# Constant products into unread accumulator columns, and one batch's q and k transposed by DMA, in an attention + gated-MLP kernel

## The chip, the cores and the metric

The kernel runs on one core of one Trainium2 chip. Its metric is device time in microseconds (us) of one execution. Executions come in a faster and a slower state, so times are compared among fast runs; square brackets behind a ratio give its 95% interval. A profiled execution gives the span that the profile covers, about 1.7 us less than the run's time. Engines: TensorE (PE, with its weight loads PEld), VectorE (DVE), ScalarE (ACT), GpSimd (POOL) and SyncE (SP, which here only issues DMAs).

## The reference, cut to what matters

Four batches; eight heads of 64; 768 positions. Attention with a window of 128 and four sink positions, then a gated MLP whose gate mixes positions:

```python
scores = q @ k.T / 8            # kept where j < 4 (sink) or 0 <= i - j < 128
a = softmax(scores); x = concat_heads(a @ v)          # 768 x 512 per batch
h = gelu(x @ w_in); u, v = h[:, :512], h[:, 512:]     # input projection
v_s = w_sg @ (layernorm(v) * g_ln) + b_sg             # mixes positions
out = x + (u * v_s) @ w_out
```

## The kernel before

The kernel is one list of steps in a fixed order. Every engine runs its own instructions in the order in which the list names them; a step that waits holds up all that stand behind it on its engine. `TQ.b.p` transposes q of batch b, head pair p on PE, `EQ` evacuates it (the last letter names the engine: A, D or P), `QK` are scores, `MV`/`MU` the two halves of the input projection, `OU` output groups, `LQ`/`LK`/`LV` loads issued by POOL, `CQ`/`CK`/`CV` casts, `HM.n` means n constant products that compute nothing and keep PE's clock up.

```python
def HM(n): pre[0] = n                       # remembered, run by the next new accumulator tile
def fresh(ring, key):
    t = ring.new(key)
    for _ in range(pre[0]):                 # 512 columns each, into the tile of the next real work
        nc.tensor.matmul(t ..., iden, ks_sink[1][:, 0:512], start=True, stop=True)
    pre[0] = 0
    return t
DT = ()                                     # batches whose q and k go through DMA transposes: none
mm_ring = Ring("mm", 4, [128, 512], F32, psum)      # four accumulator tiles, in turn
q32, k32 = Ring(..., 2, F32); qn, kn = Ring(..., 2, BF16)   # the row-order path, unused before
q16, k16 = Ring(..., 3, [128, 4, NT, Dh], BF16)     # three buffers; the load casts f32 to bf16
def LQ(b, i): return rows(q32, q, b, i) if b in DT else load(q16, q, b, i)   # 2 or 4 heads a load
def turned(dst, name, src, b, p, e):        # EQ, EK
    if b in DT: return nc.sync.dma_start_transpose(out=dst.new((b, p)), in_=src[b, p])
    copy(e, dst.new((b, p)), psb((name, b, p)))      # evacuate PE's transpose
```

A buffer of a ring can be written again only when its last reader is done, so a load waits for the work that reads its buffer's previous content.

The softmax here doesn't subtract the row's maximum and nothing guards it: scores larger than these inputs give would overflow.

## Time and profile before

| | kernel before |
|---|---|
| time, median of 3 | 168.97 us (167.69 to 170.52) |
| profiled span | 165.8 us |
| first input projection, batch 0 / first MU group of batch 1 / of batch 2 / last matmul | 29.28 / 82.33 / 106.40 / 160.93 us |
| last load of q, k or v lands | 79.52 us |

I use those four moments as stage borders: **startup**, **middle** (29.28 to 106.40, in two parts) and **tail**. The row of the page that shows the DMA engines' busy tenths in 40 slices of 4.1 us, in the kernel before: loads run without a break to slice 19 (79 us).

```profile
DMA  4999999999999998799000005901110475111055
```

The table by stage for what follows the startup, kernel before (columns: start:end, length, then busy us and instructions of PE, weight load, DVE, ACT, POOL, then PE clock, DMA share, GB/s): PE is busy nearly all the time in each stage; DVE is busy 45.12 + 21.72 = 66.8 of the middle's 77.1 us.

```profile
29.28:82.33 53.05, 52.11 (x668) 32.18 (x666) 45.12 (x97) 46.50 (x57) 40.07 (x49) 1.00 1.04 223
82.33:106.40 24.07, 24.07 (x275) 14.86 (x274) 21.72 (x54) 18.74 (x23) 9.84 (x14) 1.00 0.21 47
106.40:160.93 54.53, 54.53 (x397) 30.45 (x395) 42.57 (x99) 25.93 (x30) 15.03 (x21) 1.00 0.28 81
```

### The profile page before, as it was taken

What the parts mean: (1) busy time and instruction counts of PE and PEld (TensorE: products, weight loads), DVE (VectorE), ACT (ScalarE), POOL (GpSimd) and SP (SyncE); (2) the same over time, 40 slices, a digit from 0 to 9 for tenths busy, and PEclk for the clock granted to TensorE, in tenths of its full rate; (3) what the DMA queues carried; (4) which work ended last, traced back from release to release, by engine and by line L of the source; (5) the groups of instructions that cost most, each with busy time, mean ns of one, the idle gap of its engine ahead of it and who ended that gap; (6) DMA issues with size and microseconds to landing.
All of it is one profiled execution on the core that took longest, in us unless ns stands there. A gap on an engine that the chain in (4) does not pass through costs nothing.

```text
span 165.8 us, 4047 instructions
## 1 busy us (share of the span) xinstructions
PE 154.3 (93%) x1630; PEld 90.2 (54%) x1630; DVE 131.8 (79%) x302; ACT 110.2 (66%) x132; POOL 90.4 (54%) x123
## 2 busy tenths in 40 slices
PE   5599698999899999999999999999999999999990
PEld 1253446656565677665666575545567654555530
DVE  4179979389889989987997999838999963888861
ACT  3748966949998886999879748966676404590000
POOL 8999679646896999895240394321216610212400
PEclk9959999999999999999999999999999999999999
DMA  4999999999999998799000005901110475111055
GB/s 160 199 201 255 207 210 210 203 291 218 252 244 243 261 217 267 106 240 315 10 6 0 0 4 95 255 34 63 63 63 4 95 88 211 53 65 63 0 190 190
DMA packets 23249, 24.26 MB, mean 146 GB/s; under 512 B 8000, under 2 KB 18496, under 8 KB 23232
## 3 DMA queue, kind: packets, MB, share of 16 engines
q0 software_dynamic: 12128, 14.94, 46.5%
q1 hardware_dynamic: 11104, 9.08, 18.5%
q8 instruction: 12, 0.20, 0.5%
q14 instruction: 5, 0.04, 0.1%
HBM read 24.81 MB, written 6.29 MB: 188 GB/s over the span
## 4 chain that ended last, share of the span: by engine, by line
PE 68%; DVE 2%; DVEq 0%; issue 0%
PE mm L507 19%; PE mm L524 12%; PE sc L444 9%; PE sc L486 9%; PE sc L358 6%; PE mm L308 5%; PE mm L398 3%; PE mm L404 2%; PE mm L408 2%; DVE P L373 1%; PE mm L427 1%; PE mm L344 1%; DVEq L576 0%; DVE ot L528 0%; DVE gtmp L512 0%
## 5 line engine op out<-in xcount | busy, mean ns | idle before, releaser
L366 ACT ACTIVATE P<-sc 128x1024 bf16<-128x1024 f32 (+1 forms) x48 | 44.2, 968 | 10.8 <-PE sc L358 10.7
L507 PE MATMUL mm<-wsgT,z 128*128 128x384 bf16 x192 | 33.9, 327 | 0.7 <-DVE wsgT L502 0.7
L377 POOL TENSOR_SCALAR_AFFINE_SELECT P<-P 128x512 bf16<-128x512 bf16 x21 | 14.1, 669 | 23.0 <-ACT P L366 22.8
L507 PEld LDWEIGHTS <-z 128*128 128x128 bf16 x192 | 17.9, 98 | 13.4 <-issue 2.5
L528 DVE TENSOR_TENSOR ot<-mm,x_sb 128x512 f32<-128x512 f32 x24 | 16.3, 688 | 9.0 <-PE mm L524 8.8
L524 PE MATMUL mm<-w_out_sb,wsg_gated 128*128 128x512 bf16 x96 | 23.4, 380 | 0.0
L512 DVE SCALAR_TENSOR_TENSOR gtmp<-mm,g_sb,b_bc 128x384 bf16<-128x384 f32 x32 | 19.2, 613 | 4.4 <-PE mm L507 2.8
L486 PE MATMUL sc<-xT,w_in_sb 128*128 128x384 bf16 x128 | 22.6, 326 | 0.0
L444 PE MATMUL sc<-w_in_sb,xT 128*128 128x512 bf16 x96 | 22.2, 380 | 0.0
L373 DVE TENSOR_TENSOR P<-P,mask 128x1024 bf16<-128x1024 bf16 (+1 forms) x27 | 18.9, 718 | 1.4 <-ACT P L366 1.3
L517 POOL TENSOR_TENSOR wsg_gated<-gtmp,uT 128x384 bf16<-128x384 bf16 x13 | 12.9, 998 | 12.9 <-DVE gtmp L512 11.6
L492 ACT ACTIVATE uT<-sc 128x768 bf16<-128x768 f32 x16 | 12.7, 807 | 10.4 <-PE sc L486 10.4
L199 POOL DMA_DIRECT2D v<-in_v_dram x16 | 17.0, 1064 | 4.2 <-DVE gtmp L512 1.4
L418 DVE TENSOR_TENSOR x_sb<-mm,rcp 128x384 bf16<-128x384 f32 x32 | 17.8, 558 | 1.1
L448 ACT ACTIVATE vt<-sc 128x1024 f32<-128x1024 f32 x12 | 12.3, 1025 | 8.5 <-PE sc L444 7.7
L457 DVE BATCH_NORM_STATS2 st<-vt 128x6 f32<-128x512 f32 x24 | 16.2, 674 | 2.1 <-ACT vt L448 2.0
L465 POOL TENSOR_TENSOR rs<-rs,neg_half 128x4 f32<-128x4 f32 (+1 forms) x8 | 6.9, 864 | 19.4 <-DVE rs L460 17.5
L486 PEld LDWEIGHTS <-w_in_sb 128*128 128x128 bf16 x128 | 12.3, 98 | 8.4
L398 PE MATMUL mm<-v_sb,P 128*128 128x65 bf16 x192 | 16.4, 194 | 0.2 <-DVE P L373 0.2
L398 PEld LDWEIGHTS <-P 128*128 128x128 bf16 x192 | 14.3, 98 | 4.1 <-issue 1.5
L358 PE MATMUL sc<-qT,kT 64*128 64x256 bf16 x192 | 15.5, 269 | 0.1
L404 PE MATMUL mm<-v_sb,P 128*128 128x65 bf16 x160 | 15.4, 194 | 0.0
(75 smaller groups left out, 255.1 us busy)
## 6 DMA issues: line engine op xcount, KB each, us to landing
v<-in_v_dram POOLq DMA_DIRECT2D x16, 384.0 KB, 9.6
out_dram<-ot SPq DMA_DIRECT2D x24, 256.0 KB, 2.4
q<-in_q_dram POOLq DMA_DIRECT2D x6, 384.0 KB, 11.4
k<-in_k_dram POOLq DMA_DIRECT2D x6, 384.0 KB, 12.4
wsg_gated<-in_moe_w_sg_dram POOLq DMA_DIRECT2D x1, 1152.0 KB, 14.8
w_in_sb<-in_moe_w_in_dram POOLq DMA_DIRECT2D x2, 512.0 KB, 9.0
q<-in_q_dram POOLq DMA_DIRECT2D x3, 192.0 KB, 7.0
k<-in_k_dram POOLq DMA_DIRECT2D x3, 192.0 KB, 7.4
```

Of the source, the lines that this page charges most:

```text
L199: return nc.gpsimd.dma_start(out=ring.new((b, p)).rearrange("p h t d -> p (h t) d"), in_=src[b, 2 * p:2 * p + 2].rearrange("h (t p) d -> p ...
L358: nc.tensor.matmul(sc[:, hl, 256 * jl:256 * jl + n], kT[b, p][rows, 128 * j:128 * (j + 1)], qT[b, p][rows, 128 * j:128 * j + n], start=Tru ...
L366: nc.scalar.activation(out=pt[:, :, 0:w], in_=sc_ring[b, p, g][:, :, 0:w], func=AF.Exp, scale=scale)
L373: nc.vector.tensor_mul(pt[:, :, 0:w], pt[:, :, 0:w], m.unsqueeze(1).to_broadcast([128, 2, w]))
L398: nc.tensor.matmul(av[:, il, hl, :], P[b, p, i // 2][:, hl, 256 * (i % 2):256 * (i % 2) + 128], vb[:, h, i, :], start=first, stop=False)
L404: nc.tensor.matmul(av[:, il, hl, :], P[b, p, j // 2][:, hl, 256 * (j % 2) + 128:256 * (j % 2) + 256], vb[:, h, j, :], start=False, stop=False)
L418: nc.vector.tensor_mul(xs[:, 3 * half:3 * half + 3, 128 * p:128 * (p + 1)].rearrange("p t (h d) -> p t h d", h=2), av[:, :, :, 0:Dh], rcp. ...
L444: nc.tensor.matmul(hp[:, jl, :], xT[b][:, j, c, :], w_in_sb[:, c, d_half:2 * d_half], start=(c == 0), stop=(c == KD - 1))
L486: nc.tensor.matmul(hp[:, n, 0:NH], w_in_sb[:, c, 128 * dc:128 * (dc + 1)], xT[b][:, 3 * hf:3 * hf + 3, c, :], start=(c == 0), stop=(c == K ...
L507: nc.tensor.matmul(ps[:, 0:NH], z[b][:, si, 128 * dc:128 * (dc + 1)], wsgT[:, si, NH * hf:NH * (hf + 1)], start=(si == 0), stop=(si == NT ...
L512: nc.vector.scalar_tensor_tensor(out=gtmp.new((b, hf, dc)), in0=mm_ring["g", b, hf, dc][:, 0:NH], scalar=g_sb[:, dc:dc + 1], in1=b_bc[:, N ...
L524: nc.tensor.matmul(ps, gatedT[:, (2 * b + hf) % 3, dc, 128 * tl:128 * (tl + 1)], w_out_sb[:, dc, :], start=(dc == 0), stop=(dc == KU - 1))
```

## The change

It has three intents: constant products should stop standing in front of real work; PE should lose the 96 transposes of batch 3's q and k, which DMA does instead; and the step list is a new order fitted to both.

```diff
-DT = ()
+DT = (3,)
-    q16, k16 = Ring(..., 3, ...)
+    q16, k16 = Ring(..., 2, ...)
     def HM(n):
-        pre[0] = n
+        i = (mm_ring.used - 1) % len(mm_ring.tiles)      # the tile used last
+        while i in whole:                                # tiles all of whose columns are read
+            i = (i - 1) % len(mm_ring.tiles)
+        for _ in range(n):
+            nc.tensor.matmul(mm_ring.tiles[i][:, 390:512], iden, ks_sink[1][:, 0:122], start=True, stop=True)
 ... (fresh only keeps the set `whole`; the two loads of LG change places)
 STEPS, new order. Extracts:
-... LV.1.3 LG WT.1 LQ.2.0 XE.0.2.A ... GV.0.0 LK.2.0 MV.0.1        (loads of batch 2, early)
+... EX.1.0.1 LQ.2.0 CV.1.1.P ... EQ.2.0.A LK.2.0 GT.0.1.1        (late)
-... TK.3.3 GV.1.1 TK.3.2 BN.1.0 TQ.3.2 TQ.3.3 EK.3.3.A ...
+... CQ.3.0.P ... EQ.3.0 MV.1.0 ... LQ.3.2 ... LK.3.2 CQ.3.1.D ... LK.3.3 ... LV.3.3 ...
-HM groups: 7 2 2 6 1 7 1 (26 products of 512 columns)
+HM groups: 35 6 7 2 7 21 6 1 5 5 11 4 9 9 3 12 4 5 1 (153 of 122 columns)
```

## The prediction

> **What bounds the kernel now.** I read three things in this order: the page's busy shares and slices, then one table of busy time by stage, then the chain of waits. The first two lines say that TensorE is the busy engine and nearly always at full clock; the third is the chain that ended last.
>
> ```profile
> PE 154.3 (93%) x1630; PEld 90.2 (54%) x1630; DVE 131.8 (79%) x302; ACT 110.2 (66%) x132; POOL 90.4 (54%) x123
> ...
> PEclk9959999999999999999999999999999999999999
> ...
> PE 68%; DVE 2%; DVEq 0%; issue 0%
> ```
>
> The page warns that a busy PE is not a PE at its peak, so I cut the span at the first product of each batch's input projection (29.28 us for batch 0, 75.39 for batch 1, 106.56 for batch 2, 134.38 a little before batch 3) and at the last chain product (160.48). Columns: start:end, length, then busy us (instructions) of PE, weight load, DVE, ACT, POOL, then PE clock, DMA share, GB/s.
>
> ```profile
> 0.00:29.28 29.28, 23.20 (x296) 12.75 (x297) 20.94 (x53) 19.08 (x24) 25.43 (x41) 0.94 1.06 206
> 29.28:75.39 46.11, 45.17 (x586) 28.28 (x584) 39.56 (x86) 39.83 (x50) 37.07 (x46) 1.00 1.13 234
> 75.39:106.56 31.17, 31.17 (x358) 18.86 (x356) 27.44 (x65) 25.57 (x30) 13.00 (x19) 1.00 0.27 73
> 106.56:134.38 27.82, 27.82 (x251) 16.28 (x250) 23.61 (x58) 17.46 (x20) 9.52 (x14) 1.00 0.20 60
> 134.38:160.48 26.10, 26.10 (x144) 13.88 (x142) 18.35 (x40) 8.30 (x10) 5.35 (x6) 1.00 0.34 97
> 160.48:165.80 5.32, 0.83 (x4) 0.20 (x2) 1.89 (x3) 0.00 (x0) 0.00 (x0) 0.95 0.50 187
> ```
>
> From 29.28 us on PE is busy almost without a hole. To see whether that is real work, I took the spacing of matmul starts: 216 ns for 512 columns, 163 ns for 384, 56 ns for 128, 29 ns for 65, so 2.4 columns per ns. By that rate all matmuls need 136 us, 5.5 of it the constant products. Up to 28 us there are 11.4 us of holes between the starts; from there to 160 us again only about 11.4 us, in small pieces (0.5 to 0.7 us of each 4 us while attention and MLP mix, 0.05 in the MLP alone). So there are two regimes: a **startup** of 29 us in which PE waits for loads, DVE and ACT, and 131 us in which **PE throughput** sets the pace. The last 5.3 us is the final add and store. PE work removed after 29 us should come off the time nearly one for one, as long as DVE (86%, 88%, 85% busy in the middle stages) lets it.
>
> **What the Trainium skill says.** (1) "DMA: Bandwidth & Descriptors", section "DMA Transpose (X-bar)": 2-byte types only, hence the casts; and "Rules for kernel authors" there: "A transpose next to ordinary DMAs needs nothing", so the new ones need not wait for loads. The trace has four transposes, all with no load in flight, so it gives a size and no contention. (2) "TensorE: Matmul & The Clock Gate", Part 1: the clock is halved after an idle window of about 3.4 us. The trace agrees: a record of 3.413 us at half clock from 8.5 to 11.9 us, after a window with 1.64 us of PE busy in 3.40. (3) Part 4 of that page gives about 275 ns for a transpose in context and says such work does not engage the clock. Here twelve of them take 0.36 to 0.46 us in the chain, about 31 ns each, because they pipeline; I use the measured figure.
>
> **The change, part by part.**
>
> *Batch 3's q and k leave PE.* Its 8 groups of 12 transposes are in these chain pieces (start, us, what; the first also holds one group of batch 2):
>
> ```profile
> 69.47 0.79 PE mm L308 x24
> ...
> 79.20 1.46 PE mm L308 x48
> ...
> 98.52 1.12 PE mm L308 x36
> ```
>
> Batch 3 is half of the first and all of the other two: 0.40 + 1.46 + 1.12 = **3.0 us** of PE, all on the PE-bound path. Also gone are its 8 evacuations: 6 on ACT (0.80 to 0.82 us) and 2 on DVE (0.95). Added are 8 casts of 128x768 from f32, sized by the casts of v of the same shape: 4 on DVE at 0.64 us, 2 on POOL at 0.93, 2 on ACT at 0.87, 6.2 us in all against 6.8 us of evacuations. The transposes go to SP's queue:
>
> ```profile
> xT<-x_sb SPq DMA_TRANSPOSE x4, 3.7
> ```
>
> That is 3.7 us to landing for 128x1536 bf16, with 1.4 us of issue. The new ones are half that; I estimate 2 to 3 us each, 8 x 0.75 = 6 us of issue. In the kernel before, loads end at 79 us, and batch 3's scores start at 100 us. With loads of batch 3 through a ring of two f32 buffers they may end at 85, the transposes at 92 to 95. Still hidden. Row order costs no extra DMA time per source byte: v packets (already row order) took 0.216 us for 4096 bytes, q and k packets 0.083 us for 1536 source bytes, both about 19 GB/s on an engine.
>
> *Constant products.* Before, 26 products of 512 columns write into the tile of the next real work, so they wait for it to come free and then stand ahead of that work:
>
> ```profile
> 20.99 1.67 PE L184 MATMUL sc<-ks_sink,iden 128*128 128x512 bf16 x7 [1.54 <-ACT P L366]
> 22.60 0.39 PE L358 MATMUL sc<-qT,kT 64*128 64x256 bf16 x4
> ```
>
> Seven wait 1.54 us for ACT, then run 7 x 0.215 = 1.5 us, and only then come the scores; ACT stands idle 1.39 us for them. The same happens with six at 11.95 (ACT idle 0.81) and two at 9.13 us (about 0.9). That is some 3 us of ACT idle. After, 153 products of 122 columns write columns that nobody reads, so they wait for nothing and run in the waits. They need 153 x 51 ns = 7.8 us against 5.5, but the startup has 11.4 + 5.5 = 17 us that is not real work. The half-clock window should go. I count half of the 3 us, because DVE is 98 to 100% busy from 12 to 20 us: **1.5 us**.
>
> *The order and the engines.* Three small v-sink builds (DVE, 0.17 to 0.8 plus 0.69 us each) move out of the startup into the PE-bound stages. Two output groups (4 x 216 ns each) move from before batch 2's projections to after, neutral. Counting the list with the group means: DVE +5.5 us in all (7 more casts, 4 more masks, 3 more normalisations, fewer evacuations and products), to about 137; ACT -7 to 103; POOL +5. In the stages 29 to 106 us DVE then has about 42 + 29 us of work, for about 44 + 28 us of PE time. That is tight, so I take **1.0 us** back.
>
> Sum: span 165.8 - 3.0 - 1.5 + 1.0 = 162.3 us. The profiled run's time was 167.54, 1.7 above its span: **164.0 us**.
>
> **Rivals.** (a) *DVE becomes the bound from 75 to 106 us.* For it: 88% busy already, and its work rises while PE's falls. Against: much of it can shift by some us, and ACT is relieved. It would leave the gain at 0 to 2 us, 165.5 to 167. (b) *SP's queue blocks.* The transposes of batch 2's activations stand behind the 8 new ones, and those behind casts and late loads. If the last landed after about 100 us, PE would wait at batch 2's projection for the difference; for it the ring of two; against, some 20 us of slack between the end of loads and that use. Time 166 to 169. (c) *The startup gains nothing*, because loads bound it (DMA share above 1 from 4 us to 64 us): 165.5. (d) *The startup gains all*, clock and 3 us of ACT idle: 161.5 to 162.5.
>
> **Range and chances.** The runs before lie at 167.69, 168.97 and 170.52, wide for a fast state; I guess the startup clock differs from run to run, which denser products would steady, in favour of the change. Against the median of 168.97, 2% is 165.6. The prediction is 2.9% below. Eight in ten: 161.3 to 167.3. Faster by over 2%: 0.70; within 2%: 0.27; slower: 0.03.
>
> **What would show it.** Right: transposes by PE at 288 each of matmul and load instead of 384, no PE hole before batch 3's scores or batch 2's projection, the stages from 75 us on 2 to 3 us shorter by PE work; full clock from about 5 us; first projection at 27 to 28 us instead of 29.28; DVE near 137 us. Wrong: PE waits for DVE in the middle stages, chain share of DVE well above 2%; a PE wait ended by a DMA transpose; constant products on the chain after 20 us; or the first projection no earlier than 29 us.

## The result, and the profile after

| | before | after |
|---|---|---|
| time, median of 4 | 168.33 us (167.67 to 170.52) | 179.89 us (178.88 to 180.3) |
| ratio after / before | | 1.069 [1.062, 1.075] |
| profiled span | 165.8 | 177.2 |
| stages: startup, middle, tail | 29.28, 77.12, 54.53 | 34.91, 80.73, 56.27 |
| last load lands | 79.52 | 103.52 |

The change made the kernel 6.9% slower. Ratios are the mean time of one kernel's fast runs over that of the other's fast runs of the same rounds, so they are not quite the ratios of the medians quoted.

The page of the kernel after, the lines that answer to those shown of before: PE's share fell from 93 to 88%, the chain now has 14% of DMA and 10% each of DVE and POOL, and the DMA row has a hole from slice 11 to 14 (of 4.4 us each, so 44 to 62 us) and is then full to slice 24, 106 us.

```profile
PE 155.3 (88%) x1649; PEld 95.3 (54%) x1661; DVE 135.8 (77%) x311; ACT 104.7 (59%) x123; POOL 95.1 (54%) x123
...
PEclk9999999999999999999996999999999999999998
DMA  5999999999251299999999994952241454111054
...
PE 59%; DMA 14%; DVE 10%; POOL 10%; issue 3%; ACT 1%; DVEq 1%; POOLq 0%; ACTq 0%
```

The same stages after. Startup +5.63 us at full clock, middle +3.61 although PE has less to do, tail +1.74.

```profile
0.00:34.91 34.91, 24.35 (x427) 19.97 (x431) 23.08 (x58) 18.64 (x23) 25.53 (x40) 1.00 1.11 213
34.91:86.61 51.70, 50.04 (x599) 30.36 (x601) 44.15 (x98) 41.26 (x49) 32.30 (x37) 1.00 0.86 173
86.61:115.64 29.03, 24.50 (x230) 13.67 (x230) 23.91 (x58) 19.84 (x24) 17.76 (x21) 0.94 1.01 158
115.64:171.91 56.27, 56.06 (x401) 31.32 (x403) 43.34 (x99) 24.91 (x28) 19.54 (x26) 1.00 0.31 100
```

The tail is quickly told: two output groups, 8 matmuls of 216 ns = 1.73 us, moved into it from the middle. So the middle lost 1.7 us of that and some 2.6 us of transposes (their columns by 2.4 per ns), and was still 3.6 us longer.

**Startup.** PE's waits of the startup, in the trace of the kernel after (total us, times, longest): constant products (L183, line 183 of the kernel's file) wait for DVE and ACT.

```profile
PE mm L183 <- DVE x_sb L424: 2.2, 2, 1.3
...
PE mm L183 <- ACT kT L226: 1.9, 2, 1.0
```

One place in PE's timeline, kernel after: fifteen products wait 1.03 us for the evacuation of k, whose values they don't need, and then run 1.18 us in front of the work behind them.

```profile
22.73 1.18 PE L183 MATMUL mm<-ks_sink,iden 128*128 128x122 bf16 x15 [1.03 <-ACT kT L226]
```

The columns are indeed read by nobody, but they lie in the tile that was used last, and the program as built makes PE wait until that tile's reader is done. With a free choice of four tiles, the form took the one that is free last.

**Middle.** The chain of waits of the kernel after has two landings of k in it, with POOL's casts and issues around them:

```profile
73.21 13.50 DMA k<-in_k_dram
88.90 1.06 POOL v L204
89.96 1.01 POOL q L204
90.97 10.94 DMA k<-in_k_dram
```

The two f32 buffers that the last two loads of batch 3's q and k need were cast and free at 85.8 and 87.6 us. But these loads stand in POOL's order behind a cast of k, which itself waited 1.48 us for a landing at 86.71 us, behind a cast of v and behind an issue of v, so they go out at 89.96 and 90.97 us. Casts that wait for late loads stand in ACT's order ahead of the gelus of batch 1's projection, so PE waits for a free accumulator; timeline of PE, kernel after:

```profile
89.97 1.46 PE L492 MATMUL sc<-xT,w_in_sb 128*128 128x384 bf16 x8 [1.54 <-ACT vt L454]
93.61 4.44 PE L492 MATMUL sc<-xT,w_in_sb 128*128 128x384 bf16 x16 [2.18 <-ACT uT L498]
```

Behind that hole in PE's work also lies the only stretch below full clock before the last slice (slice 22 of the clock row): a record of 3.41 us at half clock, 93.75 to 97.16 us, so some 1.7 us of PE's work lost (an estimate, half of it). The transposes, estimated at 2 to 3 us each, took this long to land (medians of those whose landing the view could match, three of the four of q and one of the four of k; the third line is what was there before, with no load in flight):

```profile
qT<-qn SPq DMA_TRANSPOSE x4, 11.6
kT<-kn SPq DMA_TRANSPOSE x4, 4.3
xT<-x_sb SPq DMA_TRANSPOSE x4, 3.8
```

Those issued beside loads needed 7.4 to 13.6 us, with up to 4.1 us of issue on SP; the three issued from 102.5 us on, as the last load landed (103.52 us) or after it, 2.75 to 4.3 us. (For those that the view did not match, I took the semaphores in the trace.)

### The profile page after: what moved, and what is told of

It is laid out like the page before. It is cut to its first block, busy times and chain, and to the rows that moved or that the text cites. A ratio compares the mean times of both kernels' runs of the same rounds, so it can differ in the third digit from the quotient of the medians.

```text
span 177.2 us, 4108 instructions
## 1 busy us (share of the span) xinstructions
PE 155.3 (88%) x1649; PEld 95.3 (54%) x1661; DVE 135.8 (77%) x311; ACT 104.7 (59%) x123; POOL 95.1 (54%) x123
## 4 chain that ended last, share of the span: by engine, by line
PE 59%; DMA 14%; DVE 10%; POOL 10%; issue 3%; ACT 1%; DVEq 1%; POOLq 0%; ACTq 0%
DMA k<-in_k_dram 14%; PE mm L513 14%; PE sc L492 9%; PE sc L450 9%; PE mm L530 9%; PE mm L183 7%; PE mm L314 4%; PE sc L364 3%; POOL v L204 3%; DVE x_sb L424 2%; POOL q L204 2%; PE mm L404 2%; DVE gtmp L518 1%; DVE P L379 1%; POOL v_sb L229 1%
## 5 line engine op out<-in xcount | busy, mean ns | idle before, releaser
L492 PE MATMUL sc<-xT,w_in_sb 128*128 128x384 bf16 x128 | 24.6, 343 | 3.8 <-ACT uT L498 2.2
L523 POOL TENSOR_TENSOR wsg_gated<-gtmp,uT 128x384 bf16<-128x384 bf16 x18 | 18.1, 1008 | 13.4 <-DVE gtmp L518 13.3
L530 PE MATMUL mm<-w_out_sb,wsg_gated 128*128 128x512 bf16 x89 | 22.5, 379 | 0.6 <-DVE wsg_gated L523 0.2
L379 DVE TENSOR_TENSOR P<-P,mask 128x1024 bf16<-128x1024 bf16 (+1 forms) x31 | 22.3, 732 | 0.4 <-ACT P L372 0.3
L183 PE MATMUL mm<-ks_sink,iden 128*128 128x122 bf16 x153 | 12.7, 234 | 10.3 <-DVE x_sb L424 2.2
L471 POOL TENSOR_TENSOR rs<-rs,neg_half 128x4 f32<-128x4 f32 (+1 forms) x8 | 7.0, 872 | 26.8 <-DVE rs L466 24.1
L383 POOL TENSOR_SCALAR_AFFINE_SELECT P<-P 128x512 bf16<-128x512 bf16 x17 | 12.5, 735 | 15.5 <-ACT P L372 15.3
L492 PEld LDWEIGHTS <-w_in_sb 128*128 128x128 bf16 x128 | 12.9, 102 | 13.9 <-issue 5.8
L404 PE MATMUL mm<-v_sb,P 128*128 128x65 bf16 x192 | 16.6, 194 | 1.0 <-DVE ot L534 0.5
L183 PEld LDWEIGHTS <-iden 128*128 128x128 bf16 x153 | 10.6, 107 | 12.4 <-issue 10.4
```

Source lines behind the costliest of these rows:

```text
L183: nc.tensor.matmul(mm_ring.tiles[i][:, 390:512], iden, ks_sink[1][:, 0:122], start=True, stop=True)
L379: nc.vector.tensor_mul(pt[:, :, 0:w], pt[:, :, 0:w], m.unsqueeze(1).to_broadcast([128, 2, w]))
L404: nc.tensor.matmul(av[:, il, hl, :], P[b, p, i // 2][:, hl, 256 * (i % 2):256 * (i % 2) + 128], vb[:, h, i, :], start=first, stop=False)
L492: nc.tensor.matmul(hp[:, n, 0:NH], w_in_sb[:, c, 128 * dc:128 * (dc + 1)], xT[b][:, 3 * hf:3 * hf + 3, c, :], start=(c == 0), stop=(c == K ...
L523: (nc.vector if e == "D" else nc.gpsimd).tensor_mul(gatedT[:, (2 * b + hf) % 3, dc, :], gtmp[b, hf, dc], uT[b][:, dc, NH * hf:NH * (hf + 1)])
L530: nc.tensor.matmul(ps, gatedT[:, (2 * b + hf) % 3, dc, 128 * tl:128 * (tl + 1)], w_out_sb[:, dc, :], start=(dc == 0), stop=(dc == KU - 1))
```

## The experiments

Eighteen kernels ran. Stage figures are of the profiled run of each; profiles of e2, e4, e7a and e11 fell in the slow state, so their stages are only used where another run agrees.

### Which part costs the startup

**e1_no_products**: the kernel after with no constant products at all.

```diff
     def HM(n):
-        (choice of a tile and n products)
+        return
```

> The kernel after with all 153 constant products left out. Theory P (each group of products waits until DVE or ACT has read the tile that it writes beside, and holds up the real work behind it): the first input projection comes at 29 to 31 us instead of 34.90, and the time falls from 179.9 to 174 to 176.5. Rival C (the products keep the clock up and the slow startup comes from the new order of steps): the first projection stays at 34 us or later, a half-clock record appears in the startup, time 179 or more.

Measured: 176.75 us, ratio 1.049 [1.036, 1.061]. The first projection came at 27.73 us instead of 34.91: the products cost the startup 7 us. But only 3 us of it showed in the time; the middle grew, to a batch-2 projection at 113.8 us. The trace shows one reason: 10.2 us of its middle ran at half clock, against 3.4 us in the kernel after. Note also that 27.73 us, without any product, is as early as any kernel with products below starts.

**e2_next_tile**: the same products, into the tile that will be used next, which has been free for longest.

```diff
-        i = (mm_ring.used - 1) % len(mm_ring.tiles)
+        i = mm_ring.used % len(mm_ring.tiles)
         while i in whole:
-            i = (i - 1) % len(mm_ring.tiles)
+            i = (i + 1) % len(mm_ring.tiles)
```

> The kernel after with the same 153 products written to the tile that comes up next instead of the one used last, so that its readers are long done (built, 4 of the groups still wait for a reader, against 8). Theory P: first projection at 30 to 32 us, time 174 to 177.5, clock full from 5 us on. Rival (the 7.8 us of product time itself is what delays, not the wait): first projection stays within 1 us of 34.9, time 179 to 181.

Measured: 173.30 us, a median of four runs of which two are slow (the fast ones took 171.92 and 172.05), ratio 1.021 [1.002, 1.039]; first projection at 27.96 us (and 27.0 to 28.0 in all later kernels with this form, in the fast state). One index is worth some 8 us end to end among fast runs (179.89 to 172.0). So it is not the number of products (153 as before) but the tile they name. What the startup gained over the 29.28 us of before can't be put down to the products, though: e1 has none and starts as early, so it comes with the new order.

**e3_before_products**: the kernel before with only the new form of the products (four of 122 columns for each of 512), still in the tile used last. **e11_before_next_tile**: the same, in the next tile.

```diff
 (kernel before, its own step list and DT = ())
-        pre[0] = n   ... and 512-column products in fresh()
+        for _ in range(4 * n): matmul(mm_ring.tiles[i][:, 390:512], ...)   # e3: i = last; e11: i = next
```

> The kernel before with only the new form of the products: each of its 26 products of 512 columns becomes 4 of 122 columns in the tile used last. Theory P: they wait for that tile's reader, the first projection moves from 29.28 to 31 to 33 us, and the time rises from 168.3 to 170 to 172. Rival (the new form is harmless or better, as the prediction had it): 29.3 us or earlier, time 166.5 to 168.5.

> The kernel before with the 26 products in the new form (4 of 122 columns each) but in the next tile. Theory P (what costs is the wait for the reader): first projection at 28 to 29.5 us against 29.28 in before and 31.76 with the products in the tile used last, time 167 to 169.5, the same as before within 1%. Rival (any products of the new form cost): 171 to 172.5 as with the tile used last.

Measured: e3 172.04 us, 1.019 [1.005, 1.032], first projection at 31.76 us, later stages as before (53.06 and 24.06). e11 170.98 us, 1.014 [1.006, 1.021], which missed its expectation: aiming at the next tile did not make the new form a gain in the order of before. Its profile is of the slow state and starts the projection at 34.3 us, so where it loses stays open. The startup of the unchanged list varied from 28.5 to 31.0 us between kernels that share it (e7a, e7b, e12), which is as much as is at stake.

### Which part costs the middle

**e4_three_buffers**: the kernel after with three q16 and k16 buffers again. **e5_loads_early**: that, and the loads of batch 2 and of the first half of batch 3 put as early in POOL's order as before.

```diff
-    q16, k16 = Ring(..., 2, ...)
+    q16, k16 = Ring(..., 3, ...)          # e4 and e5
-... EX.1.0.1 LQ.2.0 ... EQ.2.0.A LK.2.0 ... LQ.3.0 ... LK.3.0 ...
+LG LQ.2.0 LK.2.0 ... TK.1.1 LK.2.1 LQ.3.0 LK.3.0 LQ.3.1 LK.3.1 ...   # e5 only
```

> The kernel after with three buffers again for the bf16 q and k, all else as it is. The trace of after has a hole in the loads from 44 to 60 us. Theory B (the missing third buffer makes the hole): the hole closes, loads end before 90 us instead of 102, time 173 to 176. Theory L (the load instructions stand behind other work in POOL's order, so the buffer alone frees little): the hole shortens by 1 to 3 us at most, time 178 to 180.

> The kernel after with three bf16 buffers and the loads of batch 2 and of the first half of batch 3 issued as early in the order of steps as the kernel before has them; products as in after. Theory L (late loads hold up the middle stage, because casts of batch 3 stand in the order of ACT and DVE ahead of MLP work): the hole in the loads at 44 to 60 us is gone, loads end at 85 to 92 us instead of 103.5, the stage from first projection of batch 0 (34.9) to that of batch 2 shrinks from 80.7 us to 75 to 78, time 173 to 177. Rival T (the transposes beside the loads are what costs, however early): the stage stays within 1.5 us of 80.7, time 178.5 or more.

Measured: e4 190.07 us (179.96 to 191.71, no ratio; three of the four runs are slow, and the fast one, 179.96, equals the kernel after); the load of k of batch 2 was still issued at 59.6 us. The hole in the loads therefore comes from the place of the load in POOL's order, not from the third buffer. e5 177.34 us, 1.054 [1.046, 1.063]: the hole is gone, and the loads still end at 103.9 us. That end must be read from where the middle begins: in this run the first projection came at 37.70 us, 2.8 later than in the kernel after, so the loads ended 66.2 us behind it instead of 68.6, and the middle took 77.95 us instead of 80.73. So early loads and the third buffer took some 2.8 us off the middle, and the startup of this run hid it. That the two f32 buffers pin the end of the loads is not shown: with deep ones (e8, below) loads still ended 67.4 us behind the first projection.

**e6_batch3_on_pe**: e4 (three buffers, late loads) with batch 3 back on PE.

```diff
-DT = (3,)
+DT = ()          # and TQ.3.p / TK.3.p put back where the DMA transposes stood
```

> The kernel after with q and k of batch 3 loaded as bf16 and transposed by TensorE as in before (three bf16 buffers, transposes and evacuations at the steps where after issues its DMA transposes); order, hole and products as in after. Theory: the late batch-3 casts and transposes cost more than the 3.0 us of PE they save, so this is faster than after: 172 to 176. Rival (the middle stage loses by the load hole alone): PE gets 3.0 us more work, time 181 to 184.

Measured: 193.66 us and a wrong output (relative error 1.47). My edit was at fault: eight more tiles drawn from the ring of four accumulators at those places overwrote tiles that were still to be read. Nothing follows from its time.

**e7a_before_dma**, **e7b_before_dma_late**: the DMA part alone on the order of before, with all transposes right behind the casts (a) or those of the first half late, after the loads (b). **e12_before_dma_deep**: the same idea with four q and three k f32 buffers and batch 3's q and k loaded from SP's queue.

```diff
 (kernel before)
-DT = ()   ... TQ.3.* TK.3.* EQ.3.*.A EK.3.*.A
+DT = (3,) ... CQ.3.0.D EQ.3.0 LQ.3.2 CK.3.0.A EK.3.0 LK.3.2 ...       # e7a; e7b: EQ/EK of pairs 0, 1 behind NM.1.2
+q32: 4, k32: 3; nc.sync.dma_start for LQ.3.*, LK.3.*                  # e12
```

> The kernel before, order and products kept, with only the q and k of batch 3 moved to row-order loads, casts and DMA transposes; the first half of the transposes is issued while loads still run, the second half after them (about 86 us). Theory L (with prompt loads the part is worth its PE time): 165 to 167 against 168.3 to 169.5 of before. Rival T (transposes beside loads take 7 us and more and slow both): SP or PE waits in the middle stage, 169 to 172.

> As the run before it, but all eight DMA transposes are issued after the last load (about 86 us). Theory L: 165 to 167, each transpose lands in about 2.7 us. Under rival T this one is faster than the run with early transposes by 1 us or more; under theory L alone the two agree within 0.7 us.

> The kernel before with q and k of batch 3 by row-order loads from SP's queue into four and three f32 buffers, casts placed after the loads should have landed, and DMA transposes after the last load. Theory L (with loads and casts out of the way the part is worth up to its 3.0 us of PE): loads end at 78 to 86 us, first projection of batch 2 at 103 to 106 us against 106.4, time 165 to 168.5. Rival T: projection of batch 2 at 109 us or later, time 171 or more.

Measured: 174.32 us (1.033 [1.025, 1.042]), 177.96 us (1.054 [1.045, 1.063]) and 182.21 us (1.084 [1.077, 1.091]). So the DMA part alone costs 3% and more in an order not made for it. Keeping the transposes away from the loads did not help: with either form casts placed at 86 us waited for loads that landed at 90 to 92. In e12 batch 3's loads stood in SP's queue ahead of the stores; one issue took up to 5.5 us, an output buffer did not come free, and PE stood 7.0 us at 82 us. SP's queue blocked, as in the prediction's rival (b), but by loads ahead of stores, which my own edit put there, and not by the transposes that the rival names.

**e8_deep_early**: e2's products, three q16 and k16 buffers, early loads, and four q / three k f32 buffers, so that all but one of batch 3's q and k loads go out without waiting for a cast. **e10_deep_sp**: the same with those loads from SP's queue.

```diff
+(e2's HM)
-    q32, k32 = 2 buffers;  q16, k16 = 2
+    q32 = 4, k32 = 3;      q16, k16 = 3
+LG LQ.2.0 LK.2.0 ... TK.1.1 LK.2.1 LQ.3.0 LK.3.0 LQ.3.1 LK.3.1 LQ.3.2 LK.3.2 LQ.3.3
+nc.sync.dma_start for LQ.3.*, LK.3.*        # e10 only
```

> The kernel after with products in the next tile, three bf16 buffers, the loads of batch 2 and 3 early, and four (q) and three (k) f32 buffers for batch 3 instead of two and two, so that only the last k load waits for a cast. Theory L (the end of the loads sets the first projection of batch 2, some 12 us behind it): loads end at 84 to 92 us instead of 98.6 in the run with the next-tile products alone, that projection comes at 100 to 105 us instead of 111.5, time 164 to 168. Rival T (the transposes themselves, or the casts' cost in DVE and ACT, hold the middle stage): projection of batch 2 at 109 us or later, time 171 or more.

> As the run before it, with the row-order q and k loads of batch 3 issued from SP's queue, behind the last k load of batch 2, instead of from POOL. Theory L: POOL is freed of 8 issues of about 1.06 us, loads end within 3 us of the run before it or earlier, time within 1.5 us of it, below 168. Rival (loads on two queues slow each other): loads end later than 95 us, time 170 or more.

Measured: e8 170.90 us, 1.017 [1.012, 1.021]: 9 us below the kernel after, still above before. e10 175.41 us, 1.046 [1.038, 1.055] (two of its four runs are slow; the fast ones took 173.72 and 174.33). In e10 batch 3's q and k had landed by 78.9 us (92.3 in e8), and batch 2's projection still came at 110.7 us (107.7 in e8); e12, above, and e15, below, had them by 80.1 and 78.1 us and were no faster either. So an early landing alone does not bring that projection forward. In e8 one new PE stall of 2.7 us stood at 42 us, made by the new load order. Timeline of POOL, e8: the issue of k waits 1.42 us for an older load to land, and the power for batch 0's variance (L471), on which DVE, the evacuation of w_sg and then PE wait, stands behind it.

```profile
36.62 0.76 POOL L201 DMA_DIRECT2D q<-in_q_dram  x1 [1.80 <-PE sc L492]
38.80 0.75 POOL L201 DMA_DIRECT2D k<-in_k_dram  x1 [1.42 <-DMA k<-in_k_dram]
39.56 1.72 POOL L471 TENSOR_TENSOR rs<-rs,neg_half 128x4 f32<-128x4 f32 x2
```

**e13_deep_issue_later**: e8 with those two loads issued behind that power.

```diff
-LG LQ.2.0 LK.2.0 ... RS.0.2
+LG ... RS.0.2 LQ.2.0 LK.2.0
```

> As e8_deep_early, but the loads of q and k of batch 2 are issued behind batch 0's variance power on POOL instead of ahead of it. In e8 PE stood still for 2.9 us at 42 us: DVE waited 2.5 us for that power, which stood in POOL's order behind a load issue that itself waited. Theory: that stall goes, the start of batch 1's first MU group moves from 83.6 to 81 to 82 us, and the time from 170.9 to about 168.5. Rival (DVE is full until 107 us, so what PE gains here it waits for later): start of batch 2's projection stays at 107 to 108 us and the time at 170 to 171.

Measured: 168.29 us, 1.0065 [1.000, 1.013]. The theory held in place and size (first MU of batch 1 at 80.4 us, batch 2's projection at 104.5). All that I could name as a fault by then is mended, and the changed kernel draws level with the one before, no better.

### What keeps the mended version from gaining

PE has less to do in the middle, so I set each kernel's middle beside the time its matmul columns need at 2.4 per ns (67.7 us before, 63.1 us in all forms of the change; a few records are missing in some traces, so I took the full count from e8; matmuls that fill half or a quarter of the array are counted by that share, an estimate that fits the transposes, which use half of it and took 31 ns each). The rest is stall; that of the kernel after holds the some 1.7 us lost at half clock. (Times are medians of separate sessions in which the kernel before had medians of 167.7 to 169.5 us; the ratios in the text are within one session.)

| | startup | middle | PE needs | stall in the middle | tail | time |
|---|---|---|---|---|---|---|
| before | 29.28 | 77.12 | 67.7 | 9.4 | 54.53 | 168.33 |
| after | 34.91 | 80.73 | 63.1 | 17.6 | 56.27 | 179.89 |
| e8 | 27.36 | 80.36 | 63.1 | 17.2 | 56.26 | 170.90 |
| e13 | 27.45 | 77.01 | 63.1 | 13.9 | 56.26 | 168.29 |
| e16 | 27.40 | 73.91 | 63.1 | 10.8 | 56.26 | 164.86 |
| e17 | 28.69 | 78.12 | 67.7 | 10.4 | 54.53 | 168.23 |

In e13 the 4.6 us that PE no longer needs have turned into 4.5 us of stall. The suspect is DVE, busy 72.0 of 77.0 us (94%) against 66.8 of 77.1 before.

**e14_dve_relief**: 11 copies from DVE to ACT. **e15_cast_in_load**: no casts at all; the loads of batch 3 cast, one head a load.

```diff
-CK.3.0.D CQ.3.1.D CK.3.2.D CK.3.3.D EQ.1.1.D EQ.1.2.D EQ.2.2.D XE.1.0.D XE.1.3.D Z.1.1.D Z.1.3.D
+the same, .A                                                          # e14
-rows(q32, ...), CQ.3.*, CK.3.*
+for h in range(2): nc.gpsimd.dma_start(out=qn[:, :, h, :], in_=...)   # e15, four bf16 buffers each
```

> As e13, and 11 copies of the middle stages (four casts of batch 3's q and k, three evacuations of q, two of x, two normalisations of the gate) go from DVE to ACT: by e8's own durations 8.5 us less on DVE, 9 us more on ACT. Theory (after the load and startup faults are mended, DVE, 96% busy from 45 to 108 us, bounds the middle stages): batch 2's projection starts at 102 to 105 us instead of 107.7, and the time is 165 to 167.5, level with or below the kernel before. Rival (it is the landing of the last loads and their casts, or ACT takes over as the bound): no earlier than e13, 168 to 171.

> As e13, but batch 3's q and k are cast by the load itself, one head per load straight into bf16 tiles in row order, four tiles of each, all issued early: no casts on any engine (6 us of busy time less, 3 of them on DVE) and no buffer that a load waits for. Theory (casts and f32 buffers are what the DMA part costs): loads end at or before 90 us, batch 2's projection starts at 104 to 106 us, time 166.5 to 168.5. Rival (row-order loads in 256-byte source pieces are slow on the DMA engines themselves, and DVE is full anyway): loads end no earlier than e8's 94.8 us and the time is 170 or more.

Measured: both missed. e14 169.94 us, 1.016 [1.010, 1.023]: DVE fell to 66.0 us in the middle, ACT rose to 68.6, and PE's longest waits were now for ACT: 2.5 us for exponentials, 0.9 us for evacuations. That is not a clean test: it takes from one and gives to another whose order PE also waits for. e15 172.57 us, 1.032 [1.022, 1.041]: loads ended at 95.3 us, no earlier than e8's, and the order on POOL got worse; one mask of POOL came so late that PE stood 3.8 us at 76 us.

So I made a clean one. **e16_repaired_masks_cut** takes work off DVE and gives it to nobody: the mask products of batches 1 and 2 touch only 32 columns of each half. Its output is wrong, which doesn't matter for the time. **e17_before_masks_cut** does the same to the kernel before.

```diff
     if e == "D":
         m = (mask0 if g == 0 else mask1)[:, 0:w]
+        if b in (1, 2):
+            w = 32
+            m = m[:, 0:w]
         nc.vector.tensor_mul(pt[:, :, 0:w], ...)
```

> The repaired version e13, with the 17 mask products that DVE does for batches 1 and 2 cut to the first 32 columns of each half (the output is wrong on purpose). DVE loses about 12 us (17 of 0.92 us each become about 0.2) and no other engine gets anything. Theory (DVE is what keeps the repaired version from using the time that TensorE no longer needs): batch 2's projection starts 3 to 6 us earlier than 104.5 us, at 98.5 to 101.5, and the time is 162.5 to 165.5 us, 2 to 4% below the kernel before. Rival (ACT's order and the landing of the last loads hold it, as the miss of e14 suggests): 103 us or later, 167 us or more.

> The control: the kernel before with the same cut of its 14 mask products of batches 1 and 2 on DVE (wrong output on purpose), about 8 us less on DVE. My reading of the kernel before was that TensorE bounds it from 29 us on with only about 0.5 us of stall in each 4 us: then batch 2's projection moves by 2 us at most (104.4 to 106.4) and the time is 166.5 to 169. Rival (DVE already sets part of the pace before the change): it moves by 3 us or more, and the time is under 166.

Measured: e16 164.86 us, 0.978 [0.971, 0.985], batch 2's projection at 101.3 us; e17 168.23 us, 1.000 [0.991, 1.009], at 106.8 us. The middle by stage, first e13, then e16 (third busy figure: DVE):

```profile
27.45:80.37 52.92, 49.69 (x599) 30.35 (x601) 48.50 (x103) 41.78 (x50) 39.80 (x44) 1.00 1.08 230
80.37:104.46 24.09, 22.55 (x230) 13.13 (x230) 23.50 (x57) 19.21 (x24) 13.06 (x17) 1.00 0.81 128
```

```profile
27.40:78.91 51.51, 49.55 (x599) 30.41 (x600) 43.33 (x105) 41.76 (x50) 38.02 (x44) 1.00 1.11 238
78.91:101.31 22.40, 21.84 (x230) 13.05 (x230) 20.88 (x54) 19.25 (x24) 12.84 (x18) 1.00 0.83 140
```

DVE loses 7.8 us, no other engine changes by more than 2.0 us, and the middle shrinks by 3.1 us, at the low end of what I expected. The same cut in the kernel before (4.6 us off DVE) brings nothing. So before, TensorE bounds the middle and DVE has slack; in the mended version DVE takes most of what TensorE gave up. Two things limit this. The doses differ (7.8 against 4.6 us; 17 cut masks in e16's middle against 14, from longer ones), and e16's DVE, 64.2 us in the middle, has 2.6 us less to do than that of the kernel before. And the cut also shortens each mask step, which stands in the chain from ACT's exponentials to PE: whether it was the sum of DVE's work or the length of this one step that held PE was not told apart.

**Why DVE has more to do than counted.** Mask products in the middle took 916 ns on average in e13 and 723 ns before, for the same shape; the rows of the group table over the middle (busy us, mean ns), e13 and then before:

```profile
L379 DVE TENSOR_TENSOR P<-P,mask 128x1024 bf16<-128x1024 bf16 x17 | 15.3, 916 | 0.0
```

```profile
L373 DVE TENSOR_TENSOR P<-P,mask 128x1024 bf16<-128x1024 bf16 x13 | 9.2, 723 | 0.4 <-ACT P L366 0.4
```

Six of e13's took 1.19 to 1.48 us instead of about 0.68 (two did before). Timelines of DVE and of POOL in e13 show what they share:

```profile
92.71 1.39 DVE L379 TENSOR_TENSOR P<-P,mask 128x1024 bf16<-128x1024 bf16 x1
```

```profile
92.54 1.02 POOL L523 TENSOR_TENSOR wsg_gated<-gtmp,uT 128x384 bf16<-128x384 bf16 x1
```

POOL's product ends at 93.56 us and DVE's 0.54 us later. A product of this shape takes 0.67 to 0.70 us when nothing is in its way, so most of this one fits behind POOL's end: it stood blocked for about half of its record, and the record shows busy. The Trainium skill, "SBUF — State Buffer", section "Who interferes with whom", says so: a VectorE instruction with two SBUF inputs contends with a GpSimd instruction that reads SBUF, and whoever starts second blocks until the first is done. The mask products of the middle lost 4.0 us in stretched records instead of 1.1 (each beyond 0.68 us). Of the six, four lay beside a gate product of POOL, one beside its cast of q and one beside its issues of loads; the two of before lay beside casts of v. The order of starting decides in this trace too: at 94.56 us a product of DVE started first and took its 0.67 us, and POOL's gate product beside it took 1.29 instead of 1.0. The list gives POOL five more gate products (18 instead of 13), but in the middle it runs only 7 of them in e13 and 6 in the kernel before. So the count does not explain it; the new order puts more of POOL's work beside DVE's masks. How much of it is due to gate products, casts or the order was not tested.

**e18_light_relief**: e13 with three copies moved to ACT and batch 3's v-sink build moved behind batch 2's projection.

```diff
-XE.1.0.D CK.3.0.D EQ.1.2.D ... VSM.3 (startup's end)
+XE.1.0.A CK.3.0.A EQ.1.2.A ... QK.3.2.0 VSM.3
```

> A correct version that tries to keep what e16 gained by a wrong one: e13 with only what DVE can lose cheaply. The v-sink build of batch 3 moves behind batch 2's projection, where DVE has room (0.9 us), and one evacuation of x, one of q and one cast of k go to ACT (2.3 us off DVE, 2.4 us on ACT). Theory (about 3 us off DVE, of which e16 returned some 0.4 us per us, if ACT takes three copies without becoming the wait that it was in e14): batch 2's projection at 102.5 to 104 us, time 166.5 to 168. Rival (any copy put into ACT's order delays it as in e14): 104.5 us or later, time 168.3 or more.

Measured: 168.54 us (166.23 to 168.83), 0.998 [0.990, 1.007]; batch 2's projection at 104.76 us. DVE lost only 1.7 us in the middle (70.3 us), ACT gained 2.1. (Two of the six runs are slow; the fast ones have a median of 168.2.) The rival's numbers came; its cause was not tested. No correct version that I ran beats the kernel before; what e16 gained may be there for an order that finds a home for DVE's work.

## Why the prediction was wrong, point by point

**The bound of the kernel before** was read rightly: taking 4.6 us off DVE there moves nothing (e17).

**First failed step**: "After, 153 products of 122 columns write columns that nobody reads, so they wait for nothing and run in the waits." They wait for the reader of the tile used last. In the place of 1.5 us of gain stand 5.6 us of loss; with the other tile (e2 and later) the first projection came 1.3 to 2.3 us earlier than before, about the 1.5 us predicted, but that was luck: without any product (e1) it came as early, so the gain is the new order's and not the products', and kernels that share the old order differ by more (28.5 to 31.0 us). I had looked at what data a product needs, not at which buffer it names.

**Second failed step**: "With loads of batch 3 through a ring of two f32 buffers they may end at 85, the transposes at 92 to 95. Still hidden." Loads ended at 103.5 us and the last transpose landed at 108.9. They were not hidden: casts that wait for late loads stand in ACT's order ahead of gelus, and PE waited 1.54 and 2.18 us behind them and lost some 1.7 us at half clock (an estimate). In all the middle stalled 8.2 us more than before (17.6 against 9.4). The mends up to e13 took 3.7 us of it (80.73 to 77.01; end to end also 3.7 among fast runs of e2 and e13, 2.4 by their ratios), the cut of DVE's masks 3.1 (e16), and 1.4 us is left. Early loads with the third buffer account for some 2.8 us of the 3.7 (e5, one profiled run). What the ring of two f32 buffers costs by itself stays open; deeper rings and the rest of the mends came to about 0.9 us. The size of a transpose, 2 to 3 us, was also wrong beside loads (7.4 to 13.6), though e7b gives no sign that this set the end.

"**Row order costs no extra DMA time per source byte**" fell too: row-order loads of q and k landed 1.7 to 1.9 us apart for 384 KB in e13, where before 768 KB of source took 1.8 to 2.8 us. Row-order loads of v, with the same access pattern, landed 1.0 us apart at other moments before, so the cause of it is not settled.

**A mis-sized term**: the 1.0 us that I took back for DVE. The mechanism was my rival (a), which I gave a gain of 0 to 2 us. In the mended kernel relief of DVE is worth 3.1 us (e16 against e13), two thirds of the 4.6 us of work that PE no longer has. I counted DVE's instructions by their old durations (+5.5 us; the trace of the kernel after shows +4.0), without asking what POOL's +5 us would do to those durations; in e13 DVE's total is 138.2 us, 6.4 above before.

**One reading of the clock** does not hold as it stands: the half-clock record of the kernel before runs from 8.2 to 11.6 us, not from 8.5 to 11.9, and in the 3.41 us ahead of it PE was busy 1.78 us. So the trace bears out the length of such a record, but not that the window before it was idle.

**Right**: the transposes fell from 384 to 288; the startup's half-clock stretch is gone; the two output groups are neutral (middle -1.7, tail +1.7); ACT fell by 5.5 us. That e16's 164.86 us lies near the 164.0 predicted confirms nothing: it computes something else, and its DVE has less to do in the middle than before.

## What to carry to other kernels

Filler work must be judged by the buffer that it names: do not aim it at the one that was used last, look for it in the list of waits, and try the kernel with no filler at all (here that started as early, but lost clock later). Before giving work to DMA, follow its whole supply (which buffer each load waits for, which engine's order its casts stand in), because the last link sets the end. And when the bound engine is relieved, test the next one by taking its work away for nothing, in the old kernel too: a wrong result told in two kernels what moving work about could not.

## What the Trainium skill lacked or had wrong

- "DMA: Bandwidth & Descriptors", "Rules for kernel authors": that a transpose next to ordinary DMAs needs nothing holds for the result only. Here it landed 7.4 to 13.6 us after its issue beside loads, and in 2.75 to 4.3 us as they ended or after, with up to 4.1 us of issue against 1.2.
- "TensorE: Matmul & The Clock Gate", Part 4: about 275 ns for a transpose in context is near the duration of one record here (219 ns), but not the cost of one among pipelined ones: twelve took 0.36 to 0.46 us, about 31 ns each. That Part does not give the second figure.
